# Top-k chunk attention into soft MoE: warming products of 256 columns, ten blocks of rows stored by halves, slot copies on two engines

## The chip, the cores and the metric

The kernel runs on one core of a Trainium2 chip. A core has a matrix engine (TensorE, PE in the profile), two engines for elementwise work and reductions (VectorE, DVE; ScalarE, ACT), GpSimd (POOL) and SyncE (SP), which here only issues transfers. Data are in HBM, in the on-chip memory SBUF, and in PSUM, into which TensorE writes. Sixteen DMA engines move data between HBM and SBUF; transfers are issued from SP (queue q1 in the profile) and from POOL (queue q0). The metric is the device time of one execution in microseconds (us), lower is better.

## The reference

Attention over 4 batches of 8 heads, 768 tokens of 64, where each query keeps only the 6 chunks of 32 keys with the highest upper bound; then a soft mixture of 8 experts with 4 slots each over all 3072 tokens (512 wide).

```python
ub = np.sum(np.maximum(q[:, :, :, None, :] * k_min[:, :, None, :, :], q[:, :, :, None, :] * k_max[:, :, None, :, :]), axis=-1)
ub = np.where(causal, ub, -1000000000.0)
top_chunks = np.argsort(ub, axis=-1)[..., -top_k:]
...
attn = np.exp(scores)
attn = attn / (np.sum(attn, axis=-1, keepdims=True) + 1e-09)
return np.matmul(attn, v).astype(np.float32)
...
logits = x @ phi
d = np.exp(logits - logits.max(0, keepdims=True))
d /= d.sum(0, keepdims=True) + 1e-09
slot_input = (d.T @ x).reshape(E, S_per_e, D)
for e in range(E):
    h = np.maximum(slot_input[e] @ w1[e], 0.0)
    slot_out[e] = h @ w2[e]
c = np.exp(logits - logits.max(1, keepdims=True))
c /= c.sum(1, keepdims=True) + 1e-09
return (c @ slot_out).astype(np.float32)
```

The last line makes the output: 3072 rows of 512 float32, 6.29 MB.

## The kernel before

The order of the instructions on each engine is written out by hand: lists of short words (HEAD for the start, PLAIN, REST, LOGITS, SLOTS, AFTER, BEFORE_LAST, FINAL for the sixteen pairs of heads) are walked once, and each word issues one step. Semaphore waits are added by the framework from the tiles that instructions read and write. It also keeps two engines from touching one bank of PSUM at the same time.

**The start.** `warm(n)` issues n products of a tile of ones with itself into a PSUM tile that nobody reads (`warm_ps`, 128 x 512). They stand in HEAD between the transposes and score products of the first three pairs ("w:6 w:1 ka kd ... trk:0 w:1 ..."). There are 27 of them, all before 18.5 us.

**The loads.** q, k, v and the experts' weights (float32 in HBM, bf16 on chip) are issued from POOL through q0, which runs from about 4 us on. The second-layer weights of the last two experts in the order LATE (experts 7 and 4) are loaded in eight pieces of 256 KB (`w_half`, L160): those for slot columns 256 to 511 (y = 1) first, then those for columns 0 to 255 (y = 0). They are the last loads.

**The end.** After the last pair the slots go through the experts' first layer (`experts_in`, `relu`, `hidden_T`). The second layer is done in two halves of 256 columns. For y = 1: `experts_out`, `shared_out`, `last_expert_out` sum into one PSUM bank (`outs[1]`); a copy scaled by `zinv` brings it to SBUF as the right half of `so_all` (`so_sb[1]`, on ScalarE, L1059). Then `out_half(m, 1)` for the first BYHALF = 5 entries of ROWS makes the right half of those output rows: for each 128 rows one product of transposed combine weights `cT_all` with `so_sb[1]` into PSUM, one scaling copy into `o_rows` (VectorE and ScalarE in turn, L1029 and L1026), and transfers on SP (L1050). The same follows for y = 0, with the copy of `outs[0]` on VectorE (L1068). The remaining entries of ROWS are made in whole rows of 512 columns (L1078), with one transfer for each tile (L1081).

ROWS holds (first block, blocks) with blocks of 128 rows; a tile of w blocks gives each partition w consecutive output rows, so a whole-row tile moves w times 2 KB per partition at once, while a half moves 1 KB for each row.

```python
ROWS = [(2 * m, 2) for m in range(4)] + [(8, 4), (12, 2), (14, 4), (18, 6)]
BYHALF = 5
```

So the first five tiles are 2, 2, 2, 2 and 4 blocks: twelve by halves, twelve in whole rows. After the first whole-row tile `last_rows()` runs: the combine weights of the last batch are transposed (`moe_ct`, L548 and L556), their column sums made (`col_sums`, L823) and inverted (`inv_b`), which tile (18, 6) needs. PSUM for the products comes from three pools with five places in all (tags "tp", "sc", "at").

Of the kernel before, what the change touches and what calls it, by code (L numbers as in the profile page):

```python
# [12 lines left out]
ACT = mybir.ActivationFunctionType  # L13
# [7 lines left out]
P = 128  # L21
# [38 lines left out]
def kernel(  # L60
# [10 lines left out]
    nc = tc.nc  # L71
    B, H = q.shape[0], q.shape[1]
    scale = 1.0 / (D ** 0.5)
# [38 lines left out]
    ones_sq = static.tile([P, P], BF16, name="ones_sq")  # L112
# [97 lines left out]
    warm_ps = p_at.tile([P, 4, P], F32, name="warm_ps", tag="at")  # L210

    def warm(n):
        r = ones_sq.rearrange("p (o c) -> p o c", o=1).broadcast_to([P, 4, P])
        for _ in range(n):
            nc.tensor.matmul(warm_ps, lhsT=ones_sq, rhs=r, start=True, stop=True)  # L215

    def transposes(i, nm, runs=((0, NQT),), home=(p_tp, "tp")):

# [421 lines left out]
    def head(what):  # L640
        name, *arg = what.split(":")
        if setup(name):
            return
        if name in CASTS:
            cast(*CASTS[name])
            return
        i = int(arg[0])
        if name == "w":
            warm(i)
        elif name in ("trk", "trq"):  # L650
            runs = ((0, 3), (3, NQT)) if what == "trk:0" else ((0, NQT),)
            transposes(i, name[2], runs, (p_sc, "sc") if what == "trk:0" or arg[1:] else (p_tp, "tp"))
        elif name in EVAC:
            evac_T(i, EVAC[name], *((nc.scalar.copy, nc.vector.tensor_copy) if what == "evk:0" else ()))
        elif name in DO:
            DO[name](i)
        elif name in ("lk", "lq"):
            load(i, name[1], 2)
        elif name == "sc":
            scores(0, i)  # L660
        elif name == "ex":
            expo(0, i, False)
        elif name == "mk":
            mask(0, i)
# [147 lines left out]
            return False  # L812
        return True

    ROWS = [(2 * m, 2) for m in range(4)] + [(8, 4), (12, 2), (14, 4), (18, 6)]

    def tokens(t0, w, x):
        return cT_all[:, t0:t0 + w].rearrange("p n c -> p (n c)").rearrange("p (k x) -> p x k", x=w)[:, x]
# [1 line left out]
    def col_sums(ps, b):  # L820
        cols = [(t0, w, x) for t0, w in ROWS if t0 // NQT == b for x in range(w)]
        for n, c in enumerate(cols):
            nc.tensor.matmul(ps[:, n:n + 1], lhsT=tokens(*c), rhs=live, start=True, stop=True)  # L823
# [50 lines left out]
    zinv = tail.tile([P, 1], F32, name="zinv")  # L874
# [9 lines left out]
    for n, part in enumerate((high(mneg), mneg_lo)):  # L884
        nc.tensor.matmul(
            lg2, lhsT=part.broadcast_to([NS, P]), rhs=rep.broadcast_to([NS, NQT, NS]),
            start=False, stop=(n == 1), skip_group_check=True,
        )
        nc.tensor.matmul(
            bc, lhsT=part.broadcast_to([NS, P]), rhs=ident[:NS, :NS], start=(n == 0), stop=(n == 1),  # L890
# [34 lines left out]
    so_sb = [so_all[:, y * Dm // 2:(y + 1) * Dm // 2] for y in range(2)]  # L925
    h_ps.append(p_sc.tile([P, 2, 512], F32, name="h_ps1", tag="sc"))

    def experts_in(f, g):
        for dg in range(NDG):
            for j in range(4):  # L930
                e = g * 4 + j
                nc.tensor.matmul(
                    h_ps[f][j * CH:(j + 1) * CH, 0, :], lhsT=siT_pad[:, dg, e, :],
                    rhs=w_sb[e][:, dg * F + f * 512:dg * F + (f + 1) * 512],
                    start=(g == 0 and dg == 0), stop=(g == 1 and dg == NDG - 1),
                )
# [24 lines left out]
    HD = Dm // 2  # L961
# [5 lines left out]
    outs = (so_last, so_ps)  # L967
# [37 lines left out]
    def last_expert_out(y):  # L1005
        for fg in range(NFG):
            j = fg % 4
            c0 = window(LATE[-1], j)
            nc.tensor.matmul(
                outs[y][j * CH:(j + 1) * CH, :], lhsT=hT[:, fg, c0:c0 + CH],  # L1010
                rhs=w_half[LATE[-1], y][:, fg, :],
                start=False, stop=(fg >= NFG - 4),
            )

    experts_in(0, 0)
    experts_in(0, 1)
    relu(0)
# [15 lines left out]
    BYHALF = 5  # L1033
    o_tiles = [op.tile([P, w, Dm], F32, name=f"o_rows{t0}") for t0, w in ROWS]

    def rows(m):
        t0, w = ROWS[m]
        return out[t0 * P:(t0 + w) * P, :].rearrange("(p x) d -> p x d", x=w)

    def out_half(m, y, tags):  # L1040
        cols = slice(y * HD, (y + 1) * HD)
        t0, w = ROWS[m]
        for x in range(w):
# [12 lines left out]
    experts_out(1, 1)  # L1056
    shared_out(1, 1)
    last_expert_out(1)
    nc.scalar.activation(so_sb[1], outs[1], func=ACT.Copy, scale=zinv)  # L1059
    TAGS = (("tp", "tp"), ("sc", "at"))  # L1060
    for m in range(BYHALF):
        out_half(m, 1, TAGS)
# [2 lines left out]
    for f in range(2):  # L1065
        shared_out(0, f)
    last_expert_out(0)
    nc.vector.tensor_scalar_mul(so_sb[0], outs[0], zinv)  # L1068
    for m in range(BYHALF):
        out_half(m, 0, TAGS)  # L1070

    n = 0
    for m in range(BYHALF, len(ROWS)):
        t0, w = ROWS[m]
        for x in range(w):
# [38 lines left out]
```

## Time and profile before

| What | Value |
|---|---|
| Median of three runs | 156.06 us (155.94 to 156.12) |
| The profiled execution's own time | 155.95 us |
| Its span, first to last instruction | 154.2 us |
| Busy: PE, DVE, ACT, POOL | 136.8, 120.4, 121.5, 97.5 us |
| Read from HBM, written to it | 52.49 MB, 6.29 MB |
| Software queue (q0) | 25.86 MB written on chip |
| Hardware queue (q1) | 7.08 MB |
| Warming products (L215) | 27, 8.7 us busy |
| Granted TensorE clock, mean | 0.982 |

The page shows the span in 40 slices of 3.9 us; a row of digits gives each engine's busy share in tenths. A window row gives its length, the busy time and count of each engine, the granted clock, the share of 16 DMA engines' time that packets took, and GB/s. A row of a group gives line, engine, operation, tile names and shapes, the count, then busy time and mean ns of one, then the idle time before it and what ended it. "PEld" is the loading of weights into TensorE, beside its products; "SPq" is a transfer's issue on SyncE, whose time isn't that of the transfer.

### The profile page before, as it was taken

The numbers are of one execution on the slowest core, as the hardware profiler recorded it, in microseconds if no ns is written. First come the engines' busy times: TensorE is split into PE (matmuls) and PEld (weight loads), VectorE is DVE, ScalarE is ACT, GpSimd is POOL, SyncE is SP. The second block draws the span as 40 slices with busy tenths as digits, with TensorE's granted clock in tenths as the row PEclk, the third lists the DMA queues.
The fourth block names the chain that finished last, engine by engine and source line by source line (L and its number), as shares of the span: only waits on it lengthen the run. The fifth ranks groups of instructions, "written<-read, shape, count | busy, mean of one in ns | idle before, by whom it ended". The sixth has DMA issues, their size and how long they took to land.

```text
span 154.2 us, 6098 instructions
## 1 busy us (share of the span) xinstructions
PE 136.8 (89%) x2513; PEld 91.6 (59%) x2513; DVE 120.4 (78%) x445; ACT 121.5 (79%) x167; POOL 97.5 (63%) x200
## 2 busy tenths in 40 slices
PE   7889999999999998999999799999989899776700
PEld 2444566767667686666667575767767655453300
DVE  4777988989899998999999999999767551449710
ACT  3678999999999999899999979999997133428700
POOL 6966698974976798885847938794694971000000
PEclk9999999999999999999999999999999999999975
DMA  4999999999999999999999999999999999999996
GB/s 140 207 188 206 206 189 194 215 179 196 209 217 193 199 205 189 198 205 212 205 190 198 209 202 199 206 184 213 217 191 218 211 197 198 181 266 353 371 429 255
DMA packets 45579, 33.31 MB, mean 216 GB/s; under 512 B 26224, under 2 KB 41584, under 8 KB 45296
## 3 DMA queue, kind: packets, MB, share of 16 engines
q0 software_dynamic: 41328, 25.86, 115.4%
q1 hardware_dynamic: 4224, 7.08, 12.5%
q8 instruction: 19, 0.31, 0.7%
q14 instruction: 8, 0.07, 0.1%
HBM read 52.49 MB, written 6.29 MB: 381 GB/s over the span
## 4 chain that ended last, share of the span: by engine, by line
PE 55%; POOL 13%; DMA 9%; DVE 8%; issue 5%; ACT 5%; DVEq 0%; SPq 0%; POOLq 0%; ACTq 0%
PE at_ps L382 12%; PE sc_ps L334 12%; PE sc_ps L344 9%; DMA w_half<-in_moe_w_dram 7%; PE tr_ps L225 6%; PE xT_ps L404 4%; POOL e_sb L368 4%; ACT e_sb L358 3%; PE ub_ps L284 3%; DMA w_sb<-in_q_dram 2%; PE ns_ps L316 2%; POOL v_t L174 2%; DVE o_rows L1029 2%; POOL w_half L160 1%; POOL w_sb L150 1%
## 5 line engine op out<-in xcount | busy, mean ns | idle before, releaser
L358 ACT ACTIVATE e_sb<-sc_ps 128x1024 bf16<-128x1024 f32 (+2 forms) x96 | 83.2, 932 | 4.7 <-PE sc_ps L344 4.5
L368 POOL TENSOR_SCALAR_AFFINE_SELECT e_sb<-e_sb 128x256 bf16<-128x256 bf16 x96 | 37.9, 415 | 15.6 <-ACT e_sb L358 15.2
L334 PE MATMUL sc_ps<-qT,kT 64*128 64x384 bf16 (+3 forms) x260 | 37.5, 306 | 0.7 <-ACT e_sb L358 0.6
L344 PE MATMUL sc_ps<-nsT,smask 64*128 64x384 bf16 (+2 forms) x296 | 37.6, 284 | 0.1
L382 PE MATMUL at_ps<-v_t,e_sb 128*128 128x65 bf16 x630 | 25.9, 193 | 1.0 <-DVE x_sb L395 0.8
L382 PEld LDWEIGHTS <-e_sb 128*128 128x128 bf16 x630 | 22.0, 97 | 5.1 <-issue 4.0
L305 DVE MAX8 mx<-ub_ps 128x8 f32<-128x8 f32 (+1 forms) x192 | 16.9, 165 | 5.6 <-PE ub_ps L294 5.1
L334 PEld LDWEIGHTS <-kT 64*128 64x128 bf16 x260 | 13.5, 93 | 8.4 <-issue 1.8
L174 POOL DMA_DIRECT2D v_t<-in_v_dram x16 | 16.9, 1056 | 1.1 <-PE sc_ps L344 0.9
L344 PEld LDWEIGHTS <-smask 64*128 64x128 bf16 x296 | 14.9, 95 | 3.1 <-issue 0.4
L395 DVE TENSOR_TENSOR x_sb<-at_ps,inv 128x768 bf16<-128x768 f32 (+3 forms) x18 | 15.6, 869 | 0.6
L244 DVE TENSOR_REDUCE mm<-kT 128x24 bf16<-128x768 bf16 x16 | 15.1, 944 | 0.1
L250 DVE TENSOR_REDUCE mm<-kT 128x24 bf16<-128x768 bf16 x16 | 15.1, 943 | 0.0
L235 ACT COPY qT<-tr_ps 128x768 bf16<-128x768 bf16 x16 | 13.0, 813 | 1.5 <-PE tr_ps L225 1.5
L235 ACT COPY kT<-tr_ps 128x768 bf16<-128x768 bf16 (+1 forms) x16 | 12.7, 793 | 0.6 <-PE tr_ps L225 0.6
L150 POOL DMA_DIRECT2D w_sb<-in_moe_w_dram x14 | 10.1, 724 | 0.0
L415 DVE COPY xT_sb<-xT_ps 128x768 bf16<-128x768 bf16 (+1 forms) x16 | 8.6, 535 | 2.0 <-PE xT_ps L404 2.0
L215 PE MATMUL warm_ps<-ones_sq 128*128 128x512 bf16 x27 | 8.7, 446 | 1.1 <-DVE ones_sq L180 1.1
L284 PEld LDWEIGHTS <-qpn 128*128 128x128 bf16 x192 | 6.1, 96 | 4.9 <-issue 3.8
L284 PE MATMUL ub_ps<-bd,qpn 128*128 128x48 bf16 x192 | 7.9, 184 | 0.8 <-issue 0.5
L404 PE MATMUL xT_ps<-ident,x_sb 128*128 128x128 bf16 x96 | 8.4, 220 | 0.0
L1026 ACT ACTIVATE o_rows<-oh_ps,inv_a 128x256 f32<-128x256 f32 x12 | 5.0, 470 | 3.5 <-PE oh_ps L1046 2.7
(171 smaller groups left out, 222.9 us busy)
## 6 DMA issues: line engine op xcount, KB each, us to landing
w_sb<-in_moe_w_dram POOLq DMA_DIRECT2D x14, 1024.0 KB, 18.3
v_t<-in_v_dram POOLq DMA_DIRECT2D x16, 192.0 KB, 15.1
out_dram<-o_rows SPq DMA_DIRECT2D x10, 256.0 KB, 3.0
w_half<-in_moe_w_dram POOLq DMA_DIRECT2D x8, 256.0 KB, 11.2
k_in<-in_k_dram POOLq DMA_DIRECT2D x5, 384.0 KB, 13.3
q_in<-in_q_dram POOLq DMA_DIRECT2D x5, 384.0 KB, 12.3
out_dram<-o_rows SPq DMA_DIRECT2D x1, 1536.0 KB, 6.0
out_dram<-o_rows SPq DMA_DIRECT2D x2, 512.0 KB, 3.9
```

The source lines that it names most:

```text
L174: nc.gpsimd.dma_start(out=v_t[i % NV][:, :, :, :D], in_=v[b, 2 * j:2 * j + 2].rearrange("h (g p) d -> p h g d", p=P),)
L235: copy(t.rearrange("d (p g) -> d p g", g=NQT)[:, :, g0:g1], ps.rearrange("d g p -> d p g"),)
L244: nc.vector.tensor_reduce(mm[:, 0, 0, :], kT, axis=AX.X, op=ALU.min)
L250: nc.vector.tensor_reduce(mm[:, 1, 0, :], kT, axis=AX.X, op=ALU.max)
L284: nc.tensor.matmul(o, lhsT=qpn[:, x, t * P:(t + 1) * P], rhs=bd[:, x], start=(t == 0 and x == 0), stop=False,)
L305: nc.vector.max(mx[:, a, :], ub[:, a, :max(8, 4 * t + 4)])
L334: nc.tensor.matmul(ps[:, h, c:c + w], lhsT=kT[r, kg * P:(kg + 1) * P], rhs=qT[r, qs], start=True, stop=False,)
L344: nc.tensor.matmul(ps[:, h, c + (f - t0) * P:c + (l - t0) * P], lhsT=smask[r, x, kg].rearrange("p a b -> p (a b)"), rhs=nsT[r, (f - x * NJ ...
L358: nc.scalar.activation(e[:, :, :w], st.pop(("scps", i, g))[:, :, :w], func=ACT.Exp, scale=scale)
L368: nc.gpsimd.affine_select(out=e[:, :, c:c + P], in_=e[:, :, c:c + P], compare_op=ALU.is_ge, fill=0.0, base=0, pattern=[[0, 2], [1, P]], ch ...
L382: nc.tensor.matmul(o, lhsT=st["e", i, g][:, h, c:c + P], rhs=v_t[i % NV][:, h, kg, :D + 1], start=(kg == 0), stop=(kg == t),)
L395: nc.vector.tensor_tensor(st["x", b][:, t0:t1, 2 * j:2 * j + 2, :].rearrange("p t h d -> p h t d"), at[:, :, :, :D], inv.broadcast_to([P, ...
```

## The change

`warm(n)` issues 2n products of 256 columns, in turn into the left and right half of `warm_ps`, in place of n products of 512. ROWS becomes seven tiles of two blocks and the two large ones; with BYHALF still 5, ten blocks are stored by halves, and (10, 2), (12, 2), (14, 4), (18, 6) in whole rows. `last_rows()` still follows the first whole-row tile, which is now (10, 2). A new function `slots_out(y)` copies the left 128 columns of a slot output on ScalarE and the right 128 on VectorE, and takes the place of both single copies.

```diff
     def warm(n):
-        r = ones_sq.rearrange("p (o c) -> p o c", o=1).broadcast_to([P, 4, P])
-        for _ in range(n):
-            nc.tensor.matmul(warm_ps, lhsT=ones_sq, rhs=r, start=True, stop=True)
+        r = ones_sq.rearrange("p (o c) -> p o c", o=1).broadcast_to([P, 2, P])
+        for x in range(2 * n):
+            nc.tensor.matmul(
+                warm_ps[:, x % 2 * 2:x % 2 * 2 + 2], lhsT=ones_sq, rhs=r, start=True, stop=True)
...
-    ROWS = [(2 * m, 2) for m in range(4)] + [(8, 4), (12, 2), (14, 4), (18, 6)]
+    ROWS = [(2 * m, 2) for m in range(7)] + [(14, 4), (18, 6)]
...
+    def slots_out(y):
+        w = HD // 2
+        nc.scalar.activation(so_sb[y][:, :w], outs[y][:, :w], func=ACT.Copy, scale=zinv)
+        nc.vector.tensor_scalar_mul(so_sb[y][:, w:], outs[y][:, w:], zinv)
+
...
-    nc.scalar.activation(so_sb[1], outs[1], func=ACT.Copy, scale=zinv)
+    slots_out(1)
...
-    nc.vector.tensor_scalar_mul(so_sb[0], outs[0], zinv)
+    slots_out(0)
```

## The prediction

> **What bounds the kernel now.** I read the page's slices first, then the chain of waits over the end, then the DMA in windows around the output.
>
> ```profile
> span 154.2 us, 6098 instructions
> DMA  4999999999999999999999999999999999999996
> ```
>
> The 16 DMA engines are busy in every slice from the second on. So what matters in an edit is whether it lets them run dry, and how many bytes are still to be moved when they restart. The end of the chain of waits (start, length, what):
>
> ```profile
> 127.14 10.44 DMA w_half<-in_moe_w_dram
> 137.58 0.04 issue
> 137.63 0.32 PE so_last L1009 x4
> ...
> 137.97 0.49 DVE so_all L1068
> ...
> 138.51 0.41 PE oh_ps L1046 x2
> ...
> 146.60 0.66 DVEq L1109
> ```
>
> The last half-weights land at 137.58. Only then are slot columns 0 to 255 summed (L1009), copied (L1068) and multiplied out (L1046). I call this landing the gate. The transfer took 10.44 us from its issue although it is only 256 KB: it stood behind a backlog, so compute that is late by less than that backlog doesn't move the gate. VectorE ends at 147.3 and the span at 154.2; between them there is only writing. The DMA in windows (length, engines, clock, DMA share, GB/s):
>
> ```profile
> 137.00:140.80 3.80, 2.47 (x32) 1.51 (x22) 2.38 (x6) 1.75 (x5) 0.00 (x0) 1.00 1.03 355
> 140.80:145.30 4.50, 3.43 (x23) 1.77 (x22) 3.53 (x8) 2.98 (x6) 0.00 (x0) 1.00 1.02 353
> 145.30:146.60 1.30, 0.63 (x3) 0.12 (x1) 1.30 (x3) 1.30 (x3) 0.00 (x0) 1.00 1.07 426
> 146.60:149.10 2.50, 0.00 (x0) 0.00 (x0) 0.66 (x2) 0.06 (x1) 0.00 (x0) 0.93 1.03 424
> 149.10:152.60 3.50, 0.00 (x0) 0.00 (x0) 0.00 (x0) 0.00 (x0) 0.00 (x0) 0.50 1.03 435
> 152.60:154.20 1.60, 0.00 (x0) 0.00 (x0) 0.00 (x0) 0.00 (x0) 0.00 (x0) 0.50 0.01 0
> ```
>
> The share is 1 from 137.0 to 152.6. The output queue's packets in 135.3 to 140.8, then in 135.3 to 137.0, and the queues that moved anything in 134.0 to 135.3:
>
> ```profile
> q1 hardware_dynamic: 1604, 1.57, 82.6%
> ...
> q1 hardware_dynamic: 227, 0.22, 37.6%
> ...
> q0 software_dynamic: 315, 0.16, 88.6%
> q8 instruction: 1, 0.02, 4.6%
> ```
>
> 1.57 MB is just the first half's output (12 times 128 rows of 1 KB). So 140.8 is where the first half is drained and the second begins. The windows then read: 140.8 to 145.3 the second half's twelve half-row blocks, six transfers, 0.75 us for each 256 KB; to 146.6 the first whole-row tile, 512 KB in 1.30; then 1 MB in 2.50 and 1.5 MB in 3.5. The issues on SyncE that I need:
>
> ```profile
> 134.09 0.62 SPq L1050 DMA_DIRECT2D out_dram<-o_rows  x1
> 139.44 0.53 SPq L1050 DMA_DIRECT2D out_dram<-o_rows  x1
> 145.35 0.34 SPq L1081 DMA_DIRECT2D out_dram<-o_rows  x1
> 147.33 0.33 SPq L1081 DMA_DIRECT2D out_dram<-o_rows  x1
> ```
>
> The first output is issued at 134.09, and q1 has no packet before 135.3: 1.2 us from issue to first packet. The second half's first transfer, issued at 139.44, is thus ready at 140.64, and the engines are free for it at 140.8. Both halves fit together with 0.16 us to spare. This seam is where the change acts.
>
> **The slot copies on two engines.** Each copy of 256 columns becomes 128 columns on ScalarE and 128 on VectorE. In the built program the VectorE half waits for ScalarE's, so they run one after the other. Behind it on VectorE stand the o_rows copies, which need the copy anyway. The rows for their prices (mean ns behind the busy time):
>
> ```profile
> L1026 ACT ACTIVATE o_rows<-oh_ps,inv_a 128x256 f32<-128x256 f32 x12 | 5.0, 470 | 3.5 <-PE oh_ps L1046 2.7 <-DMA w_half<-in_moe_w_dram 0.5
> L1026 ACT ACTIVATE o_rows<-o_ps,inv_a 128x512 f32<-128x512 f32 x3 | 2.0, 685 | 1.5 <-PE o_ps L1078 1.5
> L1059 ACT ACTIVATE so_all<-so_ps,zinv 128x256 bf16<-128x256 f32 x1 | 0.5, 474 | 2.2 <-PE so_ps L1009 2.2
> ...
> L1029 DVE TENSOR_SCALAR o_rows<-oh_ps,inv_a 128x256 f32<-128x256 f32 x12 | 5.2, 479 | 2.6 <-PE oh_ps L1046 2.4
> L1029 DVE TENSOR_SCALAR o_rows<-o_ps,inv_a 128x512 f32<-128x512 f32 x3 | 2.2, 748 | 0.4 <-PE o_ps L1078 0.4
> L1068 DVE TENSOR_SCALAR so_all<-so_last,zinv 128x256 bf16<-128x256 f32 x1 | 0.5, 483 | 1.8 <-PE so_last L1009 1.8
> ```
>
> ScalarE pays 685 - 470 = 215 ns for 256 columns more, so 128 fewer save 107: 474 becomes 0.36 us. VectorE pays 269, so 483 becomes 0.35. With a handover of 0.04 (as after the landing in the chain) that is 0.75 us where 0.48 stood: +0.27, twice. No row shows 128 columns, so the ends are: no saving at all on either half, 0.47 + 0.04 + 0.48, +0.51; and halves that overlap after all, 0.36, -0.13. I take +0.27, worked out from the slopes of the same two operations. No trace here shows two engines reading one PSUM bank. [...]
>
> In the first half the +0.27 delays outputs that share the engines with the last weights: in 135.3 to 137.0 they moved 0.22 MB, 0.13 per us, so 0.035 MB is left for later, 0.1 us. In the second half it lies behind the gate, on the path: first issue 139.71, ready 140.91.
>
> **Ten instead of twelve by halves.** The tile of four (8 to 11) becomes one of two by halves and one of two in whole rows. 256 KB leave the first half, where they covered the time in which the second half is being made ready, and come back behind the gate. The first half drains at 140.8 - 0.75 + 0.1 = 140.15. The second is ready at 140.91: the engines stand idle for 0.76 us. Against the 140.8 of before it starts 0.11 late, and then has one half-row transfer fewer (0.75) and a whole-row tile more (1.30): +0.55.
>
> [...] The windows differ (353 against 426 GB/s), so I keep +0.55.
>
> Do the later tiles arrive in time? The rows of VectorE in the second half, and of TensorE at the gate:
>
> ```profile
> 137.63 0.29 PE L1009 MATMUL so_last<-w_half,hT_pad 128*32 128x256 bf16 x4 [0.29 <-DMA w_half<-in_moe_w_dram]
> 138.83 2.66 DVE L1029 TENSOR_SCALAR o_rows<-oh_ps,inv_a 128x256 f32<-128x256 f32 x6 [0.38 <-PE oh_ps L1046]
> 143.88 1.41 DVE L1029 TENSOR_SCALAR o_rows<-o_ps,inv_a 128x512 f32<-128x512 f32 x2 [0.26 <-PE o_ps L1078]
> ```
>
> A pair of halves takes 2.66/6 = 0.44 us, a pair of whole rows 1.41/2 = 0.70. Everything after the halves moves by 0.27 - 0.44 = -0.17. So tile (12,2), now behind the column sums, has its last row at 143.88 + 0.75 - 0.17 = 144.46 and packets at 145.66; the engines want it at 140.91 + 3.75 + 1.30 = 145.96. The tile of four comes one whole-row pair later still: issue 145.35 - 0.17 + 0.70 = 145.88, ready 147.08, wanted 147.26. The last: 147.86, ready 149.06, wanted 149.76. All in time, the tile of four by only 0.18. The number of SyncE issues stays 14. The moe_ct block (cT, column sums) keeps its place behind the first whole-row tile and has more cover than before. In the first half TensorE does two products fewer and reaches the second half's experts 0.17 earlier; it only waits longer at the gate, where it waits 0.29 now.
>
> **Warming products.** 27 products of 512 columns become 54 of 256: the same columns, 27 weight loads more. Loads and products of the block of six, and six transposes with a load each:
>
> ```profile
> 6.68 0.98 PEld L215 LDWEIGHTS <-ones_sq 128*128 128x128 bf16 x6
> 6.69 1.47 PE L215 MATMUL warm_ps<-ones_sq 128*128 128x512 bf16 x6
> ...
> 35.58 0.33 PE xT_ps L404 x6
> ```
>
> The loads run under the products. A 128-column product with its own load takes 0.33/6 = 0.055 us; a 256-column one takes 1.47/12 = 0.12 and covers it. Cost: 0. Ends: 27 x 0.055 = +1.5 us on TensorE if no load were hidden, and no gain below 0, since the gate hangs on the DMA.
>
> **Sum.** 0.11 + 0.55 = +0.66. The profiled execution took 155.95 with a span of 154.2; that gives 156.61. It ran 0.11 under the median of 156.06, so 156.7 for the median.
>
> **Rivals.**
> Early gate (not slower): later and fewer first-half outputs let the weights land sooner. At most it returns what q1 took before 137.0, 37.6% of 1.7 = 0.64 us. Then the second half is ready at 140.27, still after the drain: -0.53 + 0.55, 156.1. For it: both queues use the same engines. Against it: the rows removed are the last of the first half and left after the landing; only the 0.27 us late start acts before it. It decides from about 0.35 us of return.
> Overlapped copies: ready at 139.44 - 0.13 + 1.2 = 140.51, drained at 140.05: -0.29 + 0.55, 156.3. Against it stands the wait in the built program.
> Starved tail: the tile of four misses its 0.18 us, because whole-row pairs behind the column sums go slower than 0.70. If both added pairs take 0.3 more, 0.42 us of idle time: 157.1. For it: ten tiles in PSUM turn in five places. Against it: the pitch of 0.70 was measured there.
> Unhidden loads: 1.5 us on TensorE, less 0.29 + 0.17 of waiting at the gate: +1.0 on top, 157.7. Against it are the rows above.
>
> **How the numbers follow.** Forecast 0.65, early gate 0.08, overlapped copies 0.08, starved tail 0.12, unhidden loads 0.04, a surprise in the first 20 us of either sign 0.03. Time: 156.7. The forecast's own range is that of the copy price: +0.26 to 0.35 + 0.55, 156.3 to 157.0. With most of the early gate and the starved tail: 156.2 to 157.2. A measurement of this kernel can't tell 0.2% (0.31 us) from none. Faster 0.05 (what is left of the early gate and the surprise); same 0.17 (both first rivals and the lower edge of the forecast); slower 0.78.
>
> **What would show it.** Right: VectorE's 128-column copy begins when ScalarE's ends; the first issue of the second half near 139.7; a stretch of some 0.7 us near 140.2 to 140.9 with a DMA share far under 1; then five half-row transfers and two tiles at about 1.3 us each; a span of about 154.9; the warming blocks as long as before. Wrong: no dry stretch, or a landing of the last weights well before 137.5, or TensorE at the gate after the weights.

## The result, and the profile after

| | Before | After |
|---|---|---|
| Median | 156.22 us (6 runs) | 158.71 us (6 runs) |
| Ratio, 95% interval | | 1.0134 (1.009 to 1.0178) |
| Span of the profiled execution | 154.2 us | 156.9 us |

The change makes the kernel 1.3% slower, about three times the forecast loss (0.4%). The seam between the two halves of the output opened as forecast, but it is less than half of the difference. The ratios, here and below, leave out executions that were held up (two of 159.2 us with the warming products alone; one of 159.74 us and one of 640.54 us, which nothing here explains, with the idle instructions), and they aren't the quotients of the medians. The page after, three of its rows:

```profile
span 156.9 us, 6146 instructions
PEclk9999999999999999999999999999999999699985
q8 instruction: 20, 0.33, 0.8%
```

The clock row has a dip in its 35th slice, and the queue that fetches instructions made 20 transfers; before there were 19. The chain of waits over the end, kernel after (start, length, what):

```profile
132.60 0.38 ACT so_all L1018
132.98 0.02 issue
133.00 0.36 DVE so_all L1019
...
135.84 1.83 PE so_last L974 x24
137.66 0.85 PE so_last L1000 x16
138.51 0.25 PE so_last L1010 x6
138.77 0.02 issue
138.79 0.38 ACT so_all L1018
139.17 0.02 issue
139.19 0.36 DVE so_all L1019
```

Each slot copy is two halves in series, 0.76 us. But TensorE's expert products now stand ahead of the second copy without a gap, where before TensorE had been waiting for the weights. The same 32 products in the timeline of before, then of after:

```profile
135.52 1.06 PE L973 MATMUL so_last<-w_sb,hT_pad 128*32 128x256 bf16 x32
```

```profile
135.77 1.90 PE L974 MATMUL so_last<-w_sb,hT_pad 128*32 128x256 bf16 x32
```

Windows of the kernel after (length, engines, clock, DMA share, GB/s) say why, and where the DMA engines ran dry:

```profile
130.00:134.50 4.50, 2.52 (x45) 1.90 (x45) 1.59 (x6) 0.99 (x3) 0.00 (x0) 1.00 1.41 192
134.50:137.90 3.40, 3.29 (x50) 1.91 (x51) 1.42 (x4) 1.61 (x4) 0.00 (x0) 0.50 1.08 252
137.90:139.40 1.50, 0.83 (x28) 0.61 (x21) 0.21 (x1) 0.37 (x1) 0.00 (x0) 0.99 1.04 365
139.40:141.70 2.30, 1.65 (x11) 1.07 (x11) 1.87 (x6) 1.68 (x4) 0.00 (x0) 1.00 0.20 70
141.70:144.70 3.00, 1.68 (x17) 0.93 (x15) 1.88 (x4) 1.05 (x2) 0.00 (x0) 1.00 1.00 336
144.70:145.20 0.50, 0.50 (x4) 0.25 (x3) 0.26 (x1) 0.47 (x1) 0.00 (x0) 1.00 0.21 70
145.20:148.50 3.30, 2.39 (x9) 0.84 (x7) 3.30 (x6) 3.11 (x6) 0.00 (x0) 1.00 1.02 395
...
154.70:155.70 1.00, 0.00 (x0) 0.00 (x0) 0.00 (x0) 0.00 (x0) 0.00 (x0) 0.50 0.07 25
```

There are three dry stretches. The seam, 139.4 to 141.7 at a share of 0.20, is 1.8 us of idle engines, where 0.76 was forecast: the granted clock was 0.50 from 134.5 to 137.9, so the products took 0.84 us longer. Then 144.7 to 145.2, which nobody forecast. And 154.7 to 155.7, at a share of 0.07 = about 1/16: one engine still takes up packets while fifteen have none left. (A window counts a packet where it starts. By the ends of the packets, the last engine is 0.77 us behind the others.) Two issues on SyncE, and the DMA queues in 142.7 to 143.0, kernel after:

```profile
140.51 0.53 SPq L1056 DMA_DIRECT2D out_dram<-o_rows  x1
```

```profile
143.14 1.37 SPq L1056 DMA_DIRECT2D out_dram<-o_rows  x1
```

```profile
q1 hardware_dynamic: 94, 0.10, 96.3%
q8 instruction: 1, 0.02, 25.3%
```

A packet of 16 KB of instructions starts on one of the sixteen engines in this window; 25.3% of 16 engines for 0.3 us is 1.2 us of one engine. The issue at 143.14 takes 1.37 us instead of 0.5 to 0.6, and the second dry stretch follows it. The engine that is late at the end may be the one that had the packet; the trace doesn't say which engine moved what, so this is argued and not shown. Added up for this execution: 0.66 forecast, 0.8 for products at half clock, 0.4 for the stretch behind the slow issue, 0.8 for the last engine; together 2.7, as the spans differ.

Theory: the 50 added TensorE instructions (27 products more in the warming, 2 fewer in the rows, and a weight load with each) bring a 20th fetch of instructions into the output phase, where no DMA engine has time to spare (fetch theory). Rivals: the seam alone costs more than was worked out (seam theory); TensorE's longer wait for the copies brings the half clock (clock theory); the short products themselves do harm in the first 20 us (warming theory).

### The profile page after: what moved, and what is told of

It reads as the page before. It is cut to its first block, busy times and chain, and to the rows that moved or that the text cites. A ratio compares the mean times of both kernels' runs of the same rounds, so it can differ in the third digit from the quotient of the medians.

```text
span 156.9 us, 6146 instructions
## 1 busy us (share of the span) xinstructions
PE 137.5 (88%) x2538; PEld 94.3 (60%) x2538; DVE 120.7 (77%) x445; ACT 121.6 (77%) x167; POOL 97.3 (62%) x200
## 4 chain that ended last, share of the span: by engine, by line
PE 49%; POOL 12%; DMA 10%; DVE 9%; ACT 7%; issue 5%; DVEq 0%; SPq 0%; POOLq 0%; ACTq 0%
PE at_ps L383 11%; PE sc_ps L335 11%; DMA w_half<-in_moe_w_dram 8%; PE sc_ps L345 8%; POOL e_sb L369 5%; PE tr_ps L226 5%; ACT e_sb L359 4%; PE xT_ps L405 3%; POOL v_t L174 2%; DVE o_rows L1035 2%; DMA w_sb<-in_q_dram 2%; PE ub_ps L285 2%; PE ns_ps L317 2%; ACT o_rows L1032 2%; POOL w_sb L150 1%
## 5 line engine op out<-in xcount | busy, mean ns | idle before, releaser
L215 PE MATMUL warm_ps<-ones_sq 128*128 128x256 bf16 x54 | 8.7, 311 | 1.1 <-DVE ones_sq L180 1.1
L309 DVE TENSOR_TENSOR ns_t<-ub_ps,mx 128x288 bf16<-128x288 f32 x16 | 7.3, 458 | 0.5
```

## The experiments

All ratios are to the kernel before on the same chip, with 95% intervals. The first four take the change apart.

**Warming products alone.**

```diff
-        for _ in range(n):
-            nc.tensor.matmul(warm_ps, lhsT=ones_sq, rhs=r, start=True, stop=True)
+        for x in range(2 * n):
+            nc.tensor.matmul(
+                warm_ps[:, x % 2 * 2:x % 2 * 2 + 2], lhsT=ones_sq, rhs=r, start=True, stop=True)
```

> The kernel before with the 54 warming products of 256 columns alone. Seam theory (the prediction's: only the dry stretch between the halves and the bytes behind the gate count): no change, ratio 1.000. Fetch theory (50 TensorE instructions more bring one more 16 KB transfer of instructions, seen at 142.7 us in the changed kernel, which holds one of the 16 DMA engines for about 1.2 us and lets its last rows land late): that transfer appears behind 140 us here too, span +0.7 to +1.3, ratio 1.004 to 1.008, and the 16 last packets of the output queue end up to 0.8 us apart instead of 0.2. Clock theory (the granted TensorE clock falls to one half for 3.4 us when TensorE waits twice ahead of the first half's products): no change, since the copies are as before.

Measured: 1.0068 (1.0036 to 1.01), median 157.65 beside 156.38. The edit that was costed at nothing makes half of the loss. It adds 54 instructions (27 products, 27 loads). The mean granted clock is no lower than that of the kernel before (0.979 and 0.978), so it isn't that the half clock came more often. SyncE's slow issue, and windows of this kernel:

```profile
142.33 1.60 SPq L1051 DMA_DIRECT2D out_dram<-o_rows  x1
```

```profile
125.70:129.10 3.40, 3.40 (x50) 1.60 (x52) 1.38 (x7) 0.70 (x2) 2.14 (x3) 0.50 1.45 198
136.10:137.40 1.30, 1.11 (x8) 0.67 (x7) 1.20 (x4) 1.23 (x4) 0.00 (x0) 1.00 0.09 12
...
143.70:144.60 0.90, 0.07 (x1) 0.07 (x2) 0.78 (x2) 0.04 (x1) 0.00 (x0) 1.00 0.13 36
```

The 20th fetch is there, at 142.2, and with it an issue of 1.60 us, behind which comes a dry stretch of 0.9 us. The part of the expectation on the last packets was a miss: here they end 0.2 us apart. The dry stretch at 136.1 stands behind a half clock at 125.7 to 129.1, in which TensorE was busy all the time, and which came without any split copy.

**Rows alone.**

```diff
-    ROWS = [(2 * m, 2) for m in range(4)] + [(8, 4), (12, 2), (14, 4), (18, 6)]
+    ROWS = [(2 * m, 2) for m in range(7)] + [(14, 4), (18, 6)]
```

> The kernel before with ten blocks by halves alone. Seam theory: first half drained at 140.05, second half ready at 140.64: starts 0.16 early, then +0.55, together +0.39 us, ratio 1.0025, with a dry stretch of 0.6 us. Fetch theory: no transfer of instructions in the output, nothing on top. Clock theory: no half clock before the output ends, nothing on top; if the half clock comes without the split copies, +0.8 on top (ratio 1.008) and the clock theory has the wrong trigger.

Measured: 1.0053 (1.002 to 1.0085). The seam theory's 1.0025 lies inside, and just so does the 1.008 that was named for a half clock without the split copies; the time doesn't tell them apart. The profiled execution had a half clock with unsplit copies, as this window shows (clock 0.50):

```profile
133.50:136.80 3.30, 2.99 (x22) 1.53 (x25) 2.34 (x5) 2.25 (x6) 0.00 (x0) 0.50 1.04 171
```

By the expectation's own words, the clock theory has the wrong trigger. A second half clock stood in this execution at 143.7 to 147.1, and behind it the share of the DMA engines fell to 0.60 at 148.0 to 148.5.

**Slot copies alone.**

```diff
-    nc.scalar.activation(so_sb[1], outs[1], func=ACT.Copy, scale=zinv)
+    slots_out(1)
...
-    nc.vector.tensor_scalar_mul(so_sb[0], outs[0], zinv)
+    slots_out(0)
```

> The kernel before with the slot copies on two engines alone. Seam theory: the second half is ready 0.27 late at 140.91, the first half still drains at 140.8 to 140.9: +0.1 us, ratio 1.0007. Clock theory: TensorE waits 0.27 longer ahead of the first half's products, the clock falls to one half over the second half's expert products, these end near 138.7 instead of 137.9 and the first transfer of the second half is issued near 140.5: about +0.9 us, ratio 1.006. Fetch theory: nothing on top.

Measured: 1.0016 (0.9983 to 1.0048). The seam theory's 1.0007 is nearest; the clock theory's 1.006 is outside.

**Rows and slot copies, warming as before.** Both diffs above.

> The changed kernel with the warming products back at 512 columns. Seam theory: +0.66 us, ratio 1.004. Clock theory: +0.66 and +0.83 for expert products at half pace, +1.5, ratio 1.0095, with a granted clock of 0.5 somewhere in 133 to 139. Fetch theory: the transfer of instructions behind 140 us is gone, and with it the late last engine (0.77) and the slow issue of 1.37 us on SyncE: about 1.2 us better than the changed kernel, whatever the clock does.

Measured: 1.0064 (1.0026 to 1.0101). Multiplied with the first experiment's ratio, 1.0064 x 1.0068 = 1.0132, this is the whole change. The seam theory's 1.004 lies inside, the clock theory's 1.0095 too; against the whole change the loss is 1.1 us smaller, where the fetch theory asked for about 1.2. The profiled execution kept full clock until 149.7 and had no fetch behind 136, so it shows the seam by itself; it is one of the two fastest of twelve (156.76 to 158.83). Its span, its first issue of the second half, and its windows:

```profile
span 155.0 us, 6092 instructions
```

```profile
139.80 0.53 SPq L1055 DMA_DIRECT2D out_dram<-o_rows  x1
```

```profile
130.00:134.50 4.50, 3.17 (x67) 2.27 (x56) 1.47 (x6) 1.21 (x4) 0.00 (x0) 1.00 1.38 186
...
139.90:141.00 1.10, 0.89 (x7) 0.52 (x6) 1.03 (x4) 1.08 (x3) 0.00 (x0) 1.00 0.25 87
141.00:145.00 4.00, 2.68 (x21) 1.39 (x19) 2.64 (x6) 2.04 (x4) 0.00 (x0) 1.00 1.03 351
145.00:153.60 8.60, 1.87 (x7) 0.62 (x5) 3.27 (x5) 2.59 (x5) 0.00 (x0) 0.77 1.01 416
```

Issue 139.80 (forecast 139.71), idle 1.1 x 0.75 = 0.83 us (0.76), restart at 141.0 (140.91), span 155.0 (154.9).

**Instructions that do nothing.** Is it the count, or what the short products do?

```diff
         if m == BYHALF:
             last_rows()
+    extra = p_tp.tile([P, 1], F32, name="extra", tag="tp")
+    for _ in range(25):
+        nc.tensor.matmul(extra, lhsT=ones_sq, rhs=ones_sq[:, :1], start=True, stop=True)
```

> The kernel before with 25 one-column products (50 TensorE instructions with their loads) behind its last output product, where TensorE has nothing left to do; their result goes nowhere. Fetch theory: the count of instructions alone brings the 20th transfer of 16 KB of instructions near 142 us, as in the kernel with the warming products alone; ratio 1.005 to 1.008. Rival, warming theory (that kernel lost by what the products of 256 columns do in the first 20 us, or by the clock behind it): no such loss here, ratio 1.000.

Measured: 1.0093 (1.0059 to 1.0127), from products that run when TensorE has nothing left to do. The fetch came at 147, later than expected. The page's row, the queues in 147.1 to 147.3, and windows to the end:

```profile
q8 instruction: 20, 0.33, 0.8%
```

```profile
q1 hardware_dynamic: 15, 0.11, 135.4%
q8 instruction: 1, 0.02, 34.2%
```

```profile
147.00:153.00 6.00, 0.08 (x4) 0.00 (x0) 0.58 (x1) 0.00 (x0) 0.00 (x0) 0.59 1.00 414
153.00:154.70 1.70, 0.00 (x0) 0.00 (x0) 0.00 (x0) 0.00 (x0) 0.00 (x0) 0.50 0.06 22
```

34.2% of 16 engines for 0.2 us is 1.1 us of one engine. All sixteen are full up to 153.0, then one takes up packets until it ends at 154.7, 1.5 us behind the others. That is the packet's length and a little more; that it is the engine with the packet is, again, argued.

**The control: as much work, few instructions.** In place of the 25, five products of 512 columns, 10 instructions.

> The kernel before with five products of 512 columns (1.1 us of TensorE, about as long as the 25 short ones) behind its last output product: 10 instructions more in place of 50. Fetch theory: the 20th transfer of instructions stays out of the output or comes after it, ratio 1.000. Rival (TensorE's work or its use of PSUM at the end is what cost 1.0093): the loss is here too.

Measured: 1.0011 (0.9974 to 1.0048). Work at that place costs nothing that can be measured; 50 instructions do. A 20th fetch is there too, but it is late: its packet starts at 156.65, when the span is over (154.9), so the page's count of 19 leaves it out. The two kernels with `idle` below have it behind their spans as well (155.7 and 155.3). The pages put it in order: with up to 2515 products on TensorE there are 19 fetches, with 2516 and 2517 the 20th comes after the end, with 2538 and 2540 it falls into the output. That points to the place of the fetch, and not to their number, as what costs. The 50 instructions with their fetch kept out of the output were not run.

**Short products, count as before.** `range(2 * n)` becomes `range(n)` in the kernel with warming products alone: 27 products of 256 columns.

> The kernel before with 27 warming products of 256 columns in place of 27 of 512: half the warming work, the same count of instructions. Fetch theory: 19 transfers of instructions, none behind 140 us, ratio 1.000. Warming theory: the loss of the 54 short products (1.007) stays or grows.

Measured: 0.9976 (0.9946 to 1.0007), 19 fetches. The short form does no harm, and half of the warming work isn't missed. The warming theory falls.

**The whole change, 27 short products.** The same edit in the changed kernel.

> The changed kernel with 27 warming products of 256 columns in place of 54, all else as changed. Fetch theory: 50 TensorE instructions fewer, no transfer of instructions behind 140 us, so the loss falls from 1.0134 to what the rows and copies cost alone, 1.004 to 1.0065, that is by 1 us. Rival (the short products themselves, or the rows and copies together with them, cost it): stays above 1.01.

Measured: 1.0065 (1.0036 to 1.0093), 19 fetches. Taking 27 products and their loads out of the first 20 us gives back half of the loss, as the fetch theory asks (1.004 to 1.0065); the interval just touches that of the whole change, and the rival's 1.01 is outside.

**Fourteen blocks by halves.** `BYHALF = 6` in the kernel before.

> The kernel before with 14 blocks by halves in place of 12 (six tiles, 2, 2, 2, 2, 4, 2). Seam theory: no dry stretch, the first half drains 0.75 later, the second half then carries one half-row transfer more (0.75) and one whole-row tile less (1.30): +0.75 - 0.55, +0.2 us, ratio 1.0013; and together with ten blocks (1.0025 by this theory) twelve is the best of the three. If instead time went with the bytes behind the gate alone, 14 would gain 0.55 us, ratio 0.9965.

Measured: 1.0017 (0.9984 to 1.0051). The seam theory's 1.0013 fits, the 0.9965 of the other does not. It isn't told from twelve.

**TensorE kept busy in its two waits.** In the kernel with rows and copies:

```diff
+    def idle(n):
+        ps = p_tp.tile([P, 4, P], F32, name="idle_ps", tag="tp")
+        r = ones_sq.rearrange("p (o c) -> p o c", o=1).broadcast_to([P, 4, P])
+        for _ in range(n):
+            nc.tensor.matmul(ps, lhsT=ones_sq, rhs=r, start=True, stop=True)
...
     slots_out(1)
+    idle(3)
...
     slots_out(0)
+    idle(3)
```

> The changed rows and slot copies with 512-column warming, and three products of 512 columns (0.64 us, their result goes nowhere) in each of TensorE's two waits of some 0.85 us for the slot copies. Clock theory (TensorE waiting there lets the granted clock fall to one half for 3.41 us in many executions, and that lies on the path): fewer such stretches between 130 and 140, mean clock up from 0.972, ratio down from 1.0064 to about 1.004. Seam theory alone: 1.004 to 1.006 with no difference to the kernel without the products. If the products hold up the first output products instead, slower.

Measured: 1.0035 (1.0006 to 1.0064) beside 1.0064. The direction is that of the clock theory, and so is the mean granted clock of the twelve executions, 0.980 beside 0.972 without these products. The fetch behind the span may hide some of it: time less span is up to 3.0 us here, at most 1.8 without them; by mean spans alone the ratio is 1.003 beside 1.007. But the intervals overlap, the two kernels ran on different chips, and the profiled execution still had a half clock, at 123.8 to 127.2. Not settled.

**A version that is a little faster than before.** Rows and copies of the kernel before, 27 products of 256 columns, `idle(2)` behind each slot copy.

> The kernel before with 27 warming products of 256 columns, and two products of 512 columns (0.43 us, result unused) in each of TensorE's two waits for the slot copies (0.57 and 0.59 us before). Clock theory: the spread of the executions comes from stretches at half clock that TensorE's idling in the tail brings on; fewer of them, mean clock above 0.981, ratio 0.993 to 0.997, below the 0.9976 of the same kernel without these products. Rival (the clock falls whatever these 0.9 us do): 0.9976, no better.

Measured: 0.9965 (0.9938 to 0.9992), median 156.32 beside 156.74. Its 12 executions lie within 0.7 us (155.96 to 156.62), the 29 of the kernel before beside it within 2.1 (156.09 to 158.21), the 12 with the short products alone within 1.5 (155.80 to 157.33). The sign that the expectation named didn't come: the mean clock is 0.981, as with the short products alone, and not above it. That it is faster than before is shown; that it is faster than the short products alone is not.

## Why the prediction was wrong

**The direction: right, but in part by luck.** "Slower" was forecast from the rows and copies, and they make about half of the loss. The other half has a cause that the prediction didn't have.

**What bounds the kernel: right.** The DMA engines are full up to the seam (share 1.04 to 1.41 from 130.0 to 139.4 after), and every loss found is a stretch in which they are not (0.07 to 0.21 after).

**Slot copies: right.** Forecast 0.75 us in series; measured 0.38, a handover of 0.02 and 0.36. VectorE waited for ScalarE, as in the built program. At full clock the first issue moved by 0.36 (139.80 against 139.44), and 0.11 of that is the weights' landing: the last products started at 137.74 there and at 137.63 before. That leaves 0.25, forecast 0.27.

**Ten blocks by halves: right.** Span +0.8 with the copies at full clock, forecast +0.66; ratio 1.0064 with an interval that holds the forecast 1.0042. The tile of four and the last tile were not starved in that execution: the share is 1.01 from 145.0 to 153.6.

**Warming products: wrong, and this is the step that failed.** "The loads run under the products ... Cost: 0." The products took as long as forecast; the row of the block of six, now twelve, in the timeline after:

```profile
6.49 1.48 PE L215 MATMUL warm_ps<-ones_sq 128*128 128x256 bf16 x12
```

That is 1.48 us against 1.47. But instructions have to be moved too: the page counts their packets (q8, 20 after, 0.33 MB) in the time of the sixteen engines. The prediction counted the DMAs that the program issues and costed the 54 added instructions by their time on TensorE only. Both bounds, "no gain below 0" and "+1.5 us if no load were hidden", were bounds of the wrong resource. The page had the row (q8, 19 transfers, 0.31 MB), and the count of products on TensorE (2513, and as many loads; 2538 of each after the change). In its place the runs showed: 54 instructions more as warming products, 1.0068; 50 more as idle ones behind the end, 1.0093; 10 more, with the 20th fetch behind the span, 1.0011; the count as before, 0.9976; the count back in the changed kernel, 1.0134 down to 1.0065.

**Rivals.** Early gate: no. In the profiled execution after, the last weights weren't even what was waited for. Overlapped copies and unhidden loads: neither happened. Starved tail: not at full clock, but in part beside a half clock in the output. With the rows alone it stood at 143.7 to 147.1, in the changed kernel with 27 products at 144.6 to 148.1, and at 148.0 to 148.5 the share fell to 0.60 and 0.39. The tile of four had only the 0.18 us to spare; the prediction priced every stage at full clock. TensorE at the gate after the weights, named as a sign of error, did happen in that execution, by the half clock.

**What stays open.** What brings the half clock on. It stood at 134.5 to 137.9 after, at 125.7 to 129.1 with the warming products alone, at 133.5 to 136.8 with the rows alone, and nowhere in the output for rows and copies together. So the split copies aren't needed for it. Ahead of it TensorE was busy for 2.52 of 4.50 us in the changed kernel, and for 3.17 in the same window of the execution that kept its clock; that would fit TensorE's idling as the cause. Other executions speak against a plain busy share: with the warming products alone the clock fell after 3.40 us of which TensorE was busy for 2.71, and with rows and copies it stayed up after 3.40 us of which it was busy for 2.04 (139.5 to 142.9). The half clock may be a part of the spread between executions of one kernel: over the 35 of the kernel before beside the first four experiments, time and mean clock have a correlation of -0.6. Of the changed kernel's 2.7 us in the profiled execution it made 0.8. Whether the change makes it more frequent wasn't shown. How one fetch costs a whole us was only seen, not tested. That an issue on SyncE takes longer beside a fetch is seen in eleven of the thirteen profiled executions: in each, one issue of the output took 0.94 to 1.60 us and overlaps a fetch (1.37 and 1.60 beside the packets at 142, and 1.42 in the kernel before, beside its fetch at 134.9), while no other took more than 0.67. But some fetches had an issue beside them that wasn't slow, so the fetch alone doesn't decide it.

## What to carry to other kernels

Here 50 and 54 instructions more brought one more transfer of 16 KB into an end that is bound by the DMA engines, and cost 0.9% and 0.7%. Where another kernel's end is bound like this, count the fetches on the page before and after an edit, and look at when the last ones come; the page doesn't count one that comes after the last instruction (with the five idle products at 156.65, the span being 154.9). Splitting the warming products in two was free on their engine here (1.48 us against 1.47 for the block of six), and still cost 0.7% of the kernel, with a fetch at 142.2, behind 4.60 us at a DMA share of 1.00. And look at what the engines have to write while the next part is made ready: with 256 KB moved from there to behind that point they stood idle for 0.83 us at the seam (rows and copies, ratio 1.0064; rows alone, 1.0053).

## What the runs showed of the hardware

One 16 KB packet of instructions in the output took 1.1 to 1.4 us of one of sixteen engines (1.1 with the idle instructions, 1.2 after, 1.4 with the warming products alone: 8.6% of 16 engines for 1.0 us), and the last engine was then 0.77 us (after) and 1.5 us (idle instructions) behind the other fifteen. With the warming products alone the sixteen ended within 0.2 us and the loss lay in a slow issue (1.60 us) and a dry stretch (0.9 us at a share of 0.13) instead. Where the packet came behind the span, with no output left to move, no loss could be measured (1.0011 for the five idle products, 0.9965 for the version with `idle(2)`). What the earlier packets cost no run tested.

The granted clock fell to one half for 3.4 us at a time (134.5 to 137.9 after, 134.4 to 137.8 with 27 products) in a tail in which TensorE still had work, once after 4.50 us in which it was busy for 2.52. The places differed between executions of nearly the same program; what sets the place and the length no run showed.
